# Turned features of tiles 8 to 15 moved inside SBUF in sixteen transfers on two queues, not through DRAM

## The chip, the cores and the metric

The kernel runs on one core of a Trainium2 chip. The metric is the time of one execution in microseconds (us) of device time; a time "of the kernel" is the median of several runs. Beside the timed runs there is one profiled execution, and all durations of single instructions come from it. The engines are called TensorE (PE; PEld is its weight load), VectorE (DVE), ScalarE (ACT), GpSimd (POOL) and SyncE (SP). SyncE and GpSimd each issue DMA transfers from a queue of their own, in order: a transfer at the head of a queue that has to wait holds up all that stand behind it.

## The reference

```python
xn = layernorm(x)                                   # x: 2048 x 512
out = x + A(xn) + B(xn)

def A(x):                                           # linear attention, 32 heads of 16
    q, k, v = heads(x @ wqkv)
    phi_q = cat(softmax(q @ w_phi), softmax(-(q @ w_phi)))    # 32 features a head
    phi_k = cat(softmax(k @ w_phi), softmax(-(k @ w_phi)))
    kv, z = phi_k.T @ v, phi_k.sum(over s)
    o = (phi_q @ kv) / (phi_q @ z + 1e-6)
    return o @ wo

def B(x):                                           # gated MLP, width 688 after the split
    z = gelu(x @ w_in)
    z1, z2 = z[:, :688], layernorm(z[:, 688:])
    return (z1 * (w_sp @ z2 + b_sp[:, None])) @ w_out
```

All is float32. The change concerns `phi_q`, divided by its denominator, on its way to the product with `kv`.

## The kernel before, in words

The 2048 rows are sixteen tiles of 128 rows (NT = 16), and a tile's query features are 128 rows by 1024 features (NF = 1024). Most products are made from three matmuls on split operands (`mm3`, lines 54 to 58: high by high, high by low, low by high), and TensorE works through four stages.

1. Projections of x to v, and to the exponentials of the key and query features. The queries' exponentials and the reciprocals of their sums are stored in DRAM as `e_d` (line 338). The gate inputs z1 are stored too.
2. The second half of the gate input, its layer norm, and its split into operands `B`.
3. The product with `w_sp` in seven partial products (`products`, line 771, tiles named `g`), up to about 489 us. After each of its eight row blocks, `gate` (line 797) makes the gated features u, turns them, and stores them in DRAM as `u_d` and `ur_d` (lines 818 and 820). In this stage the query features of tiles 0 and 1 are turned as well and stored in `q_d` (lines 886 to 891).
4. The projection stage, from about 489 us on: the loop of line 1064 over pairs of tiles, i = 0, 2, ... 14. For each pair TensorE runs `project_u(i)` (u of the first tile by `w_out`, into `pout`), then `attend` (32 small matmuls of line 997, from `kvT` and the turned features `f`, into `po`), then `project_u(i + 1)`, then `project_o` for both tiles (`oT` by `wo`, into the same `pout`). ScalarE copies `pout` to `xr`, of which there are three buffers, and GpSimd adds `xr` to the output in DRAM (line 1030). In between, ScalarE and VectorE split the next u (`uh`, `ul`) and the outcome of `attend` (`oT`, lines 1001 and 1002).

The matmuls of `attend` contract over features, so the features have to stand on partitions: each tile's 128 x 1024 block must be turned. Tiles 2 to 7 are turned on TensorE (lines 974 to 985). Tiles 0, 1 and 8 to 15 are turned on VectorE: one transpose instruction (line 561) turns all 32 x 32 blocks in place, and a DMA then has to carry the blocks to their partitions. For tiles 8 to 15 that is the branch `s >= TQ` of `features` (lines 935 to 940):

- `q_fin` (line 541) divides by the denominator, in seven VectorE instructions with `tmp` as scratch;
- `turn_q` (line 559) transposes `e` into `tmp` (tile name `qtmp`), and four DMAs on GpSimd's queue, one for each block b of 32 partitions, store it in `q_d[s]`, 128 KB each;
- one DMA on SyncE's queue loads `q_d[s]` into the half of the pair's operand tile `f`, 512 KB. It waits for the four stores.

The operand tiles `f` come from `er_pair`, which has three buffers of a pair each. `tmp` and the tile `et`, into which `e_d` is loaded, come from the rotating slots of `xz`.

The order of the work: `ahead(i)` (line 1054) asks, after the `project_o` of tile i, for the load of `et` of tile i + 5, of u of tile i + 4, and for `features(i + 3)`. In line 1087 the last `gate` is put behind pair 6; it stores the u of tiles 14 and 15. `tc.issue_after` puts instructions behind a given one on the same engine. What this does not fix is laid out by a planner, which runs through the program with simulated times (`schedule_with_timeline_sim=True`, line 1121) and from them writes the order of each engine and each queue; on the chip each engine then follows its order strictly, and waits by semaphores.

Of the kernel before, what the change touches and what calls it, by code (L numbers as in the profile page):

```python
# [10 lines left out]
F32 = mybir.dt.float32  # L11
# [7 lines left out]
P = 128  # L19
S, D, H, DH, FH = 2048, 512, 32, 16, 688  # L20
NT = S // P
# [3 lines left out]
NF = 2 * D  # L25
# [3 lines left out]
BL = 32  # L29
# [11 lines left out]
def mixer(ctx: ExitStack, tc: tile.TileContext, x, x_t, wv, wqkT, phi_bd, wo, w_in, wst, b_r, w_out, out):  # L41
    nc = tc.nc
    pe, act, dve, pool, sp = nc.tensor, nc.scalar, nc.vector, nc.gpsimd, nc.sync


    def round_h(eng, h, src):
        if eng is act:
            return act.activation(h, src, AF.Copy).ins  # L48
        return eng.tensor_copy(h, src).ins

    def rest_l(l, src, h, eng=None):
        return (eng or dve).tensor_tensor(l, src, h.bitcast(F32), op=ALU.subtract).ins  # L52
# [18 lines left out]
    def xz_tile(n, dt, name):  # L71
        return xz.tile([P, SL], dt, tag="xz", name=name)[:, :n]

    mid = ctx.enter_context(ExitStack())
    dram = ctx.enter_context(tc.tile_pool(name="dram", bufs=1, space=DRAM))
# [3 lines left out]
    ur_d = dram.tile([NT, 2 * REM, P], F32, name="ur_d")  # L79
    kvT_d = dram.tile([P, D], F32, name="kvT_d")  # L80
    zb_d = dram.tile([P, NF], F32, name="zb_d")
    q_d = dram.tile([NT, P, NF], F32, name="q_d")
    nm_d = dram.tile([NT, ND, P], F32, name="nm_d")

    ident = cst.tile([P, P], F32, name="ident")
# [91 lines left out]
    with ExitStack() as p0:  # L177
# [236 lines left out]
        t = xz_tile(2 * D, F32R, "xT").rearrange("p (a b) -> p a b", a=2)  # L414
        xT.append(t)
        x0, pts = xt.pop(0), []
        for k in range(2):
            pts.append(ps.tile([P, 2, P], F32, tag="mm", name="pt"))
            for c in range(2):
                i = pe.transpose(pts[k][:, c], x0[:, (2 * k + c) * P:(2 * k + c + 1) * P], ident).ins  # L420
            keep(pe=i)
        warm_up(2)
        for cs, pt in zip(halves, pts):
            src = pt.rearrange("p a b -> p (a b)")
            i = round_h(act, t[:, 0, cs], src)
# [7 lines left out]
        p = ps.tile([P, D], F32, tag="mm", name="proj")  # L433
# [7 lines left out]
        p = ps.tile([P, D], F32, tag="mm", name="proj")  # L441
# [18 lines left out]
        p = ps.tile([P, D], F32, tag="mm", name="proj")  # L460
# [80 lines left out]
    def q_fin(et, tmp, zb):  # L541

        e, r, t, w = et[:, :NF], *(et[:, NF + k * 2 * H:NF + (k + 1) * 2 * H] for k in range(3))
        den = et[:, NF + 6 * H:QW]
        dve.tensor_tensor(tmp, e, zb, op=ALU.mult)
        dve.tensor_reduce(t, heads(tmp), axis=AX.X, op=ALU.add)
        dve.tensor_tensor(t, t, r, op=ALU.mult)
        dve.scalar_tensor_tensor(den, pairs(t, 0), EPS_DEN, pairs(t, 1), op0=ALU.add, op1=ALU.add)
        dve.reciprocal(den, den)
        dve.tensor_tensor(w.rearrange("p (h a) -> p h a", a=2), r.rearrange("p (h a) -> p h a", a=2),  # L550
                          den.unsqueeze(2).to_broadcast([P, H, 2]), op=ALU.mult)
        return e, dve.tensor_tensor(heads(e), heads(e), bc(w, 2 * H), op=ALU.mult).ins
# [3 lines left out]
    NB = NF // P  # L556
    QB = NB * BL

    def turn_q(s, dst, e, eng):

        dve.transpose(dst.rearrange("p (m c t) -> p m c t", c=NB, t=BL), e.rearrange("p (c m j) -> p m c j", c=NB, j=BL))
        for b in range(P // BL):
            eng.dma_start(q_d[s, :, b * QB:(b + 1) * QB].rearrange("(m j) w -> j m w", j=BL),
                          dst[b * BL:(b + 1) * BL].rearrange("p (m w) -> p m w", w=QB))

    QC = 4
    NQ = NT // QC
# [45 lines left out]
    with ExitStack() as p1:  # L613
# [44 lines left out]
        for s in range(NE):  # L658
            et = load_q(s, tb.tile([P, QW], F32, name="et") if s else tmp1.tile([P, 4, D], F32, tag="zhl", name="et").rearrange("p a b -> p (a b)")[:, :QW])
            tmp = zw.tile([P, 4, FC], F32, tag="z2", bufs=2, name="qtmp").rearrange("p a b -> p (a b)")[:, :NF]  # L660
            e, _ = q_fin(et, tmp, zb)
# [57 lines left out]
    for s in range(NT):  # L719
        p = zproj((kv_ps_p, zc, zbp, za)[s % 4], s, w2, (0, 1) if s % 2 == 0 else (1, 0))  # L720
# [6 lines left out]
        z = z2[n][:, 2 * (s % 2):2 * (s % 2) + 2]  # L727
# [37 lines left out]
    def load_z1(i):  # L765
        t = gt.tile([P, 2, FH + REM], F32, tag="z1", name="z1t")
        for k in range(2):
            pool.dma_start(t[:, k, :FH], z1_d[2 * i + k])  # L768
        return t
# [27 lines left out]
    def gate(i, cb, z, u, ut, after=None):  # L797
        cb, first, _ = cb
        with tc.issue_after(after or first):
            act.activation(z[:, :, :FH], z[:, :, :FH], AF.Gelu_apprx_tanh)  # L800
        zs = z[:, :, :FH].rearrange("p k (j f) -> p k j f", j=2)
        us = u[:, :, :FH].rearrange("p k (j f) -> p k j f", j=2)
        dve.tensor_tensor(us, zs, cb, op=ALU.mult)
        lo, hi = u[:, :, KF * P:FH], u[:, :, FH:FU].bitcast(F32R)
        dve.tensor_copy(hi, lo)
        rest_l(lo, lo, hi)

        def turn():
            src = ut.rearrange("p k f -> p (k f)")
            m, r = src[:, :2 * KF * P], src[:, 2 * KF * P:]  # L810
            for k in range(2):
                dve.transpose(m[:, k * KF * P:(k + 1) * KF * P].rearrange("p (m c t) -> p m c t", c=KF, t=BL),
                              u[:, k, :KF * P].rearrange("p (c m j) -> p m c j", c=KF, j=BL))
            dve.transpose(r.rearrange("p (k f) -> p k f", k=2), u[:, :, KF * P:])
            eng = pool if i == NP - 2 else sp
            for b in range(0, P, BL):
                w = b // BL * KF * BL
                eng.dma_start(u_d[2 * i:2 * i + 2, :, w:w + KF * BL].rearrange("k (m j) w -> j (k m) w", j=BL),
                              m[b:b + BL].rearrange("p (m w) -> p m w", w=KF * BL))
                eng.dma_start(ur_d[2 * i:2 * i + 2, :, b:b + BL].rearrange("k (a j) t -> j (k a) t", j=BL),  # L820
                              r[b:b + BL].rearrange("p (a t) -> p a t", t=BL))

        return turn

    def slot(name, dt=F32):
        return xz_tile(2 * FH, dt, name)
# [40 lines left out]
    g, es, ets, ft, ep = {}, {}, {}, {}, {}  # L867
    for n in range(NC):
        i = SEQ[n][0]
        if n % NQ == 1 and i < NP - 1:  # L870
            z = load_z1(i)
        products(n, g)
        if n % NQ == NQ - 1 and i < NP - 1:
            c = gt.tile([P, 2, FU], F32, tag="c", name="c")
            cq = c[:, :, :FH].rearrange("p k (j f) -> p k j f", j=2)
            cb = drain(i, g, cq)
            g = {}
        if n + 3 < NC:
            raw[n + 3] = load_a(n + 3)
        if n + 2 < NC:  # L880
            A[n + 2] = prep_a(n + 2, raw.pop(n + 2))
        if n % NQ == NQ - 1 and i < NP - 1:
            turn = gate(i, cb, z, c, z, prep_a.last)
            if i < NP - 2:
                turn()
            if i in (2, 4):
                s = i // 2 - 1
                e, t = (gt.tile([P, 2, FU], F32, tag=tag, name=name).rearrange("p k f -> p (k f)")[:, :NF]
                        for tag, name in (("c", "c"), ("z1", "z1t")))
                pool.dma_start(e, e_d[s, :, :NF])  # L890
                turn_q(s, t, e, pool)
        if n == NC - 4:
            stage_w()
        if n == NC - 3:
            zs = slot("zb", F32R)
            zb, ident_r = zs[:, :NF].bitcast(F32), zs[:, NF:NF + P]
            round_h(act, ident_r, ident)
            sp.dma_start(zb, zb_d)
            uT = [first_gate(0)]
            ets[2] = load_q(2, slot("et"))  # L900
            es[2], last = q_fin(ets.pop(2), slot("qtmp")[:, :NF], zb)
        if n == NC - 2:
            fq = [slot("f")[:, :NF].rearrange("p (k b c t) -> p k b c t", k=2, c=NB // 2, t=BL) for h in range(2)]
            for k in range(2):
                for h in range(2):
                    sp.dma_start(fq[h][:, k], q_d[k].rearrange("p (b h w) -> h p b w", h=2, w=QB // 2)[h])
            t = xz_tile((KF + 1) * P, F32R, "u1")
            us = {1: load_u(1, t[:, :KF * P].bitcast(F32), t[:2 * REM, KF * P:(KF + 1) * P])}
    cb = drain(NP - 1, g, slot("c").rearrange("p (k j f) -> p k j f", k=2, j=2))
    with tc.issue_after(cb[2]):  # L910
        turn()
    mid.close()


# [13 lines left out]
    def features(s):  # L928
        with tc.issue_after(fin[-1]):
            tmp = slot("qtmp")[:, :NF]  # L930
            es[s], ins = q_fin(ets.pop(s), tmp, zb)
        fin.append(ins)
        if s == 3:
            return
        if s >= TQ:
            if s % 2 == 0:
                ft[s] = er_pair("f").bitcast(F32)
            turn_q(s, tmp, es.pop(s), pool)
            sp.dma_start(ft[s - s % 2][:, s % 2], q_d[s])
            return  # L940
        e = es[s]
        if s % 2 == 0:
            ep[s] = er_pair("er")
        es[s] = ep[s - s % 2][:, s % 2]
        lasts[6] = pool.dma_start(es[s].bitcast(F32), e).ins
# [117 lines left out]
    p, nxt = {}, dict(enumerate(uT))  # L1063
    for i in range(0, NT, 2):
# [17 lines left out]
        if i == 2:  # L1082
            with tc.issue_after(lasts[6]):
                z = load_z1(NP - 1)
# [40 lines left out]
```

## Time and profile before

| | before |
|---|---|
| timed runs | 619.74, 620.32, 622.54 us; median 620.32 |
| profiled execution | 618.58 us |
| its span, first to last instruction | 616.8 us |
| mean granted TensorE clock | 0.998 |
| bytes moved by DMA | 109.95 MB |
| SyncE's queue (q1, with hardware descriptors) | 43400 packets, 64.96 MB |
| GpSimd's queue (q0, with software descriptors) | 12656 packets, 38.64 MB |

How to read the views: the page's first part gives the busy time of each engine. The windows view gives it by stretches. A timeline row has the start, the duration, the engine, the line, the operation, and what it writes and reads; several equal instructions in a row are merged ("x4"), and then the duration reaches from the start of the first to the end of the last. "SPq" is SyncE's queue: the duration is that of the issue, not of the transfer. What follows in brackets is how long the engine sat idle before and what ended that. "Landing" is the time from a DMA's issue to its arrival. The chain of waits follows the work that ended last back to its start; "issue" is time in which the engine waited for nothing that the profile can name.

### The profile page before, as it was taken

Reading aid. Unit: us, or ns where it says so; the run is one execution under the profiler, and the core shown is the slowest. Engines: PE = TensorE matmul, PEld = TensorE weight load, DVE = VectorE, ACT = ScalarE, POOL = GpSimd, SP = SyncE. Lnnn points to the kernel's source line nnn. Section 1 sums busy time; section 2 is a strip of 40 time slices with the busy share of each in tenths; the row PEclk is TensorE's granted clock in tenths of the full one; section 3 lists DMA queues with packets and bytes.
Section 4 is the critical chain, followed back from the end, with each engine's and each line's share of the span. In section 5 each row is a group of like instructions: output and inputs, shape, how many; then the busy total and the mean of one; then the engine's idle time right before and its main releaser. Section 6 shows DMA issues by size and latency. Waiting matters only on the chain.

```text
span 616.8 us, 11392 instructions
## 1 busy us (share of the span) xinstructions
PE 607.8 (99%) x4286; PEld 554.4 (90%) x4286; DVE 519.0 (84%) x929; ACT 261.5 (42%) x416; POOL 134.2 (22%) x236
## 2 busy tenths in 40 slices
PE   8999999999999999999999999999999999999996
PEld 7888888888889999999999999999999987777775
DVE  5999999999978398989889896877879999999821
ACT  5653334323523467876434443342435343332221
POOL 4122232232110015442000002000100032344420
PEclk9999999999999999999999999999999999999999
DMA  8557876666446768001463745555566799999772
GB/s 315 192 136 165 227 178 170 159 163 169 125 143 162 255 224 289 2 1 35 149 142 124 191 96 177 135 157 145 165 182 215 214 345 306 322 272 264 188 172 58
DMA packets 58415, 109.95 MB, mean 178 GB/s; under 512 B 12457, under 2 KB 24617, under 8 KB 58121
## 3 DMA queue, kind: packets, MB, share of 16 engines
q1 hardware_dynamic: 43400, 64.96, 34.4%
q0 software_dynamic: 12656, 38.64, 25.1%
q10 hardware_dynamic: 2304, 5.64, 2.3%
q8 instruction: 33, 0.54, 0.3%
q14 instruction: 22, 0.17, 0.1%
HBM read 66.85 MB, written 35.80 MB: 166 GB/s over the span
## 4 chain that ended last, share of the span: by engine, by line
PE 95%; DMA 2%; issue 0%; DVE 0%; ACT 0%; SPq 0%; POOL 0%; DVEq 0%; ACTq 0%; POOLq 0%
PE g L58 11%; PE g L57 11%; PE g L56 11%; PE proj L57 7%; PE proj L56 7%; PE proj L58 7%; PE zps L56 6%; PE zps L57 6%; PE zps L58 6%; PE pout L56 6%; PE pout L58 5%; PE pout L57 5%; PE po L997 1%; DMA wst__2228<-in_w_in 1%; PE kvps L355 1%; PE pout L1011 1%
## 5 line engine op out<-in xcount | busy, mean ns | idle before, releaser
L57 PE MATMUL g<-B,A 128*128 128x344 f32 x448 | 143.3, 320 | 0.0
L56 PE MATMUL g<-B,A 128*128 128x344 f32 x448 | 142.9, 320 | 0.0
L58 PE MATMUL g<-B,A 128*128 128x344 f32 x448 | 140.4, 321 | 0.1
L56 PEld LDWEIGHTS g<-B,A 128*128 128x128 f32 x448 | 84.3, 188 | 0.1
L57 PEld LDWEIGHTS g<-B,A 128*128 128x128 f32 x448 | 84.2, 188 | 0.0
L58 PEld LDWEIGHTS g<-B,A 128*128 128x128 f32 x448 | 83.6, 188 | 0.4 <-DVE A L52 0.4
L48 ACT ACTIVATE A<-S 128x512 fp32r<-128x512 f32 x64 | 39.5, 630 | 78.7 <-DVE S L603 53.7
L56 PE MATMUL proj<-wqk_h,xT 128*128 128x512 f32 x128 | 50.1, 391 | 0.0
L58 PE MATMUL proj<-wqk_h,xT 128*128 128x512 f32 x128 | 49.8, 389 | 0.0
L57 PE MATMUL proj<-wqk_l,xT 128*128 128x512 f32 x128 | 49.8, 389 | 0.0
L123 ACT ACTIVATE e<-e,r_x 128x1024 f32<-128x1024 f32 x26 | 29.8, 1148 | 42.3 <-DVE e L122 41.2
L52 DVE TENSOR_TENSOR A<-S,A 128x512 fp32r<-128x512 f32 x64 | 43.0, 684 | 3.1 <-ACT A L48 2.8
L48 ACT ACTIVATE A<-wf 128x512 fp32r<-128x512 f32 (+1 forms) x64 | 32.9, 516 | 24.9 <-DMA wf<-in_wst 19.0
L56 PE MATMUL zps<-w_0h,xT 128*128 128x344 f32 x128 | 40.9, 320 | 0.1
L57 PE MATMUL zps<-w_1l,xT 128*128 128x344 f32 x128 | 40.8, 319 | 0.0
L57 PE MATMUL zps<-w_0l,xT 128*128 128x344 f32 x128 | 40.8, 319 | 0.0
L58 PE MATMUL zps<-w_0h,xT 128*128 128x344 f32 x128 | 40.8, 318 | 0.0
L56 PE MATMUL zps<-w_1h,xT 128*128 128x344 f32 x128 | 40.7, 318 | 0.0
L58 PE MATMUL zps<-w_1h,xT 128*128 128x344 f32 x128 | 40.6, 319 | 0.0
L52 DVE TENSOR_TENSOR A<-wf,A 128x512 fp32r<-128x512 f32 (+1 forms) x64 | 35.1, 551 | 3.7 <-ACT A L48 3.7
L126 DVE TENSOR_REDUCE sm<-e 128x64 f32<-128x1024 f32 x26 | 31.1, 1199 | 2.5 <-ACT e L123 2.5
L768 POOL DMA_DIRECT2D z1t<-z_d x16 | 8.7, 552 | 108.8 <-DMA wf<-in_wst 71.8
(224 smaller groups left out, 1435.4 us busy)
## 6 DMA issues: line engine op xcount, KB each, us to landing
wf<-in_wst SPq DMA_DIRECT2D x64, 256.0 KB, 3.2
e_d<-e POOLq DMA_DIRECT2D x16, 544.0 KB, 4.8
et<-e_d SPq DMA_DIRECT2D x16, 544.0 KB, 7.2
z_d<-z1f ACTq DMA_DIRECT2D x16, 344.0 KB, 3.1
z1t<-z_d POOLq DMA_DIRECT2D x16, 344.0 KB, 4.3
zacc<-e POOLq DMA_DIRECT2D x10, 512.0 KB, 4.9
u<-u_d SPq DMA_DIRECT2D x15, 320.0 KB, 4.9
xt<-in_x SPq DMA_DIRECT2D x16, 256.0 KB, 4.3
```

Of the source, the lines that this page charges most:

```text
L48: return act.activation(h, src, AF.Copy).ins
L52: return (eng or dve).tensor_tensor(l, src, h.bitcast(F32), op=ALU.subtract).ins
L56: pe.matmul(dst, ah, bh, start=start, stop=False)
L57: pe.matmul(dst, ah, bl, start=False, stop=False)
L58: return pe.matmul(dst, al, bh, start=False, stop=stop).ins
L123: softmax_pair.last = less, act.activation(e, e, AF.Exp, scale=scale).ins
L126: dve.tensor_reduce(sm, heads(e), axis=AX.X, op=ALU.add)
L355: i = pe.matmul(kv_acc[k:k + QP, m // 4], vs[:, m * QP:(m + 1) * QP], e[:, m * HP:(m + 1) * HP], start=first and m < 4 and len(ready) == n ...
L768: pool.dma_start(t[:, k, :FH], z1_d[2 * i + k])
L997: lasts[3] = pe.matmul(po[r][c * QP:(c + 1) * QP, k], kvT[rows, m // 2, cols], fs[m // 4][rows, m // 2 % 2], start=True, stop=True).ins
L1011: lasts[2] = pe.matmul(p, rt, w, start=False, stop=i == NT - 1 and k == 1).ins
```

## The change

For tiles 8 to 15 the four stores to `q_d` and the load from it go. In their place `move_q` copies straight from `tmp` to the operand tile: for each block b of 32 source partitions and each block m of 32 target partitions one DMA of 32 partitions by 256 elements (1 KB each, 32 KB in all). Those with b = 0 and 2 are issued on SyncE's queue, those with b = 1 and 3 on GpSimd's, so a tile has eight on each. Tiles 0 and 1 still go through `q_d`, which shrinks to two tiles. `turn_q` is divided into `turn` and `store_q`, and the function that `gate` returns is now held as `turn_u`.

```diff
-    q_d = dram.tile([NT, P, NF], F32, name="q_d")
+    q_d = dram.tile([2, P, NF], F32, name="q_d")
...
-    def turn_q(s, dst, e, eng):
-
+    def turn(dst, e):
         dve.transpose(dst.rearrange("p (m c t) -> p m c t", c=NB, t=BL), e.rearrange("p (c m j) -> p m c j", c=NB, j=BL))
+
+    def store_q(s, t):
         for b in range(P // BL):
-            eng.dma_start(q_d[s, :, b * QB:(b + 1) * QB].rearrange("(m j) w -> j m w", j=BL),
-                          dst[b * BL:(b + 1) * BL].rearrange("p (m w) -> p m w", w=QB))
+            pool.dma_start(q_d[s, :, b * QB:(b + 1) * QB].rearrange("(m j) w -> j m w", j=BL),
+                           t[b * BL:(b + 1) * BL].rearrange("p (m w) -> p m w", w=QB))
+
+    def move_q(f, t):
+        for b in range(P // BL):
+            for m in range(P // BL):
+                move_q.last = (sp if b % 2 == 0 else pool).dma_start(f[m * BL:(m + 1) * BL, b * QB:(b + 1) * QB],
+                                                      t[b * BL:(b + 1) * BL, m * QB:(m + 1) * QB]).ins
...
                 pool.dma_start(e, e_d[s, :, :NF])
-                turn_q(s, t, e, pool)
+                turn(t, e)
+                store_q(s, t)
...
         if s >= TQ:
             if s % 2 == 0:
                 ft[s] = er_pair("f").bitcast(F32)
-            turn_q(s, tmp, es.pop(s), pool)
-            sp.dma_start(ft[s - s % 2][:, s % 2], q_d[s])
+            turn(tmp, es.pop(s))
+            move_q(ft[s - s % 2][:, s % 2], tmp)
             return
```

More of the change, by code (lines that the diff above doesn't have):

```diff
@@ L882, in mixer @@
         if n % NQ == NQ - 1 and i < NP - 1:
-            turn = gate(i, cb, z, c, z, prep_a.last)
+            turn_u = gate(i, cb, z, c, z, prep_a.last)
             if i < NP - 2:
-                turn()
+                turn_u()
             if i in (2, 4):
@@ L910, in mixer @@
     with tc.issue_after(cb[2]):
-        turn()
+        turn_u()
     mid.close()
```

## The prediction, made before the result was known

> **What bounds the kernel now.** I read the page first: span, busy shares and the chain of waits.
>
> ```profile
> span 616.8 us, 11392 instructions
> ...
> PE 607.8 (99%) x4286; PEld 554.4 (90%) x4286; DVE 519.0 (84%) x929; ACT 261.5 (42%) x416; POOL 134.2 (22%) x236
> ...
> PE 95%; DMA 2%; issue 0%; DVE 0%; ACT 0%; SPq 0%; POOL 0%; DVEq 0%; ACTq 0%; POOLq 0%
> ```
>
> TensorE is busy 99% of the span and is 95% of the chain that ended last. A change that takes no matmul away can win only what TensorE idles: 616.8 - 607.8 = 9.0 us in all, start and end included. The change touches the projection stage (from 489 us on), and there only tiles 8 to 15. So next came the windows, cut from one `po` (line 997) to the next; columns are busy us and count of PE, PEld, DVE, ACT, POOL, then clock, DMA share, GB/s.
>
> ```profile
> 525.48:541.39 15.91, 15.91 (x114) 12.66 (x120) 15.47 (x22) 5.72 (x11) 5.39 (x9) 1.00 0.99 307
> 541.39:555.87 14.48, 14.48 (x99) 11.31 (x105) 14.22 (x24) 5.02 (x8) 5.25 (x9) 1.00 0.98 282
> 555.87:571.92 16.05, 14.47 (x91) 11.26 (x91) 15.78 (x23) 3.84 (x7) 6.61 (x11) 1.00 0.98 273
> 571.92:586.47 14.55, 14.55 (x98) 11.44 (x105) 12.28 (x19) 3.68 (x6) 6.12 (x10) 1.00 0.70 174
> 586.47:600.94 14.47, 14.47 (x98) 11.30 (x105) 2.98 (x5) 3.10 (x6) 4.00 (x6) 1.00 0.76 169
> ```
>
> One window has a hole: the third takes 16.05 us for 14.47 of matmuls. The others are full. The chain, in order of time, names the place:
>
> ```profile
> 569.87 0.47 PE pout L1011 x2
> 570.34 1.58 issue
> 571.92 1.10 PE po L997 x32
> ```
>
> TensorE is ready for the `po` of pair 10 (tiles 10 and 11) at 570.34 and starts at 571.92. No engine is named; the `po` reads `f`, which comes by DMA. The timelines of VectorE (the transposes, line 561), GpSimd and SyncE's queue show how late `f` is:
>
> ```profile
> 538.88 1.24 DVE L561 STREAM_TRANSPOSE qtmp<-et 128x1024 f32<-128x1024 f32 x1
> ...
> 556.93 1.24 DVE L561 STREAM_TRANSPOSE qtmp<-et 128x1024 f32<-128x1024 f32 x1
> ...
> 570.16 1.24 DVE L561 STREAM_TRANSPOSE qtmp<-et 128x1024 f32<-128x1024 f32 x1
> ...
> 585.27 1.25 DVE L561 STREAM_TRANSPOSE qtmp<-et 128x1024 f32<-128x1024 f32 x1
> ```
>
> ```profile
> 558.47 2.25 POOL L563 DMA_DIRECT2D q_d<-qtmp  x4 [4.61 <-DVE qtmp L561]
> ```
>
> ```profile
> 554.72 0.32 SPq L939 DMA_DIRECT2D f<-q_d  x1
> ...
> 558.95 0.48 SPq L820 DMA_DIRECT2D ur_d<-zt  x1
> 560.84 0.34 SPq L538 DMA_DIRECT2D et<-e_d  x1
> 563.60 0.34 SPq L836 DMA_DIRECT2D u<-u_d  x1
> 564.10 0.80 SPq L837 DMA_DIRECT2D rt<-ur_d  x2
> 564.94 0.43 SPq L836 DMA_DIRECT2D u<-u_d  x1
> 565.53 29.80 SPq L939 DMA_DIRECT2D f<-q_d  x5
> ```
>
> The four transposes are those of tiles 9, 11, 13 and 15, the second of each pair; they end at 540.12, 558.17, 571.40 and 586.52. Tile 11's stores are issued from 558.47 to 560.72, its load (the first of the x5) only at 565.53, and `po` starts 6.4 us later. So the way from transpose to operand takes 571.92 - 558.17 = 13.75 us for tile 11. Call it M. What TensorE allows before it stalls is, by pair: 8, 555.87 - 540.12 = 15.75; 10, 570.34 - 558.17 = 12.17; 12, 586.47 - 1.58 - 571.40 = 13.49; 14, 600.94 - 1.58 - 586.52 = 12.84 (the last two with the stall taken out of TensorE's clock). Pair 10 is the tightest, and 13.75 - 12.17 = 1.58 is the hole. If M were the same for every tile, the end would move by max(0, M - 12.17) - 1.58.
>
> **The change, part by part.** Removed, for eight tiles: four stores on GpSimd and one load on SyncE, and SyncE's wait between them. Added: sixteen moves of 32 partitions by 1 KB, eight on each queue, which wait for the transpose itself. The matmuls, and all up to tile 8, stay. The rows for the price come from SyncE's waits, its timeline, the answer for line 831, the answer for `q_d`, the page's DMA issues, and the answer for `er` from 500 us on:
>
> ```profile
> SPq L939 <- DMA q_d<-qtmp: 36.5, 9, 9.4
> ```
>
> ```profile
> 482.88 8.61 SPq L831 DMA_DIRECT2D wof<-in_wo  x16
> ```
>
> ```profile
> DMA to landing us min/median/max: 1.9/3.3/5.2
> ```
>
> ```profile
> L563 POOL DMA_DIRECT2D q_d<-qtmp x32: 550/572/937, 534.6 to 588.5; - x32
> ```
>
> ```profile
> u_d<-zt SPq DMA_DIRECT2D x4, 160.0 KB, 5.1
> ```
>
> ```profile
> DMA to landing us min/median/max: 5.6/7.7/9.6
> ```
>
> The waits of SyncE for `q_d` (36.5 us) go, and nothing that TensorE needs hangs on them but `f`. For the new M: issue on SyncE, 16 small loads in 8.61 us (second), 0.54 each, so 8 x 0.54 = 4.3 us; on GpSimd at the present store's 0.572, 8 x 0.572 = 4.6. Landing: the trace has no 32 KB move inside SBUF. From below, the 64 KB `wof` loads land in 1.9 at the least (third). From above, the 512 KB copy `er<-et`, the one SBUF to SBUF transfer there is, takes up to 9.6 (last). I take 5.1, of the `u_d<-zt` stores: also many small transfers by 32 partitions, in the same crowded stretch, with DMA at 0.98. SyncE stands behind those stores until 558.95 + 0.48 = 559.43, 1.3 after tile 11's transpose. M = 1.3 + 4.6 + 5.1 = 11.0, against 12.17 allowed: the hole closes, by 1.2 us of margin. The ends are 4.3 + 1.9 = 6.2 (hole gone just as well) and 1.3 + 8 x 0.937 + 9.6 = 18.4. For pairs 8, 12 and 14 the same 11.0 is under 15.75, 13.49 and 12.84, so pair 14 is late next. Gain: 1.58.
>
> One row says the queue can choke:
>
> ```profile
> SPq L538 <- DMA f<-q_d: 1.4, 1, 1.4
> ```
>
> The `et` load at 560.84 neither reads nor writes `f`, yet waited 1.4 us for an `f` load: the one at 554.72, exactly eight issues before it. I read this as at most eight transfers in flight on a queue. Tile 11's eight moves then each wait for one of the eight `u_d` and `ur_d` stores. With 5.1 us of landing these are free from 553 + 5.1 on, so this lies within the 1.3 already counted; under slower landings it does not.
>
> On GpSimd the change adds 32 issues net, 32 x 0.572 = 18 us, 4.6 per pair; it is busy 6.61 of 16.05 us in the fullest window. Queued behind its moves are the `out` accumulations, which free the three `xr` buffers:
>
> ```profile
> 551.35 0.92 POOL L1030 DMA_DIRECT2D out<-xr  x1 [0.91 <-ACT xr L1029]
> ```
>
> ```profile
> 566.56 0.60 ACT L1029 ACTIVATE xr<-pout 128x512 f32<-128x512 f32 x1 [1.04 <-PE pout L58]
> ```
>
> ```profile
> out<-xr POOLq DMA_DIRECT2D x15, 256.0 KB, 6.2
> ```
>
> The buffer written at 566.56 is that of the issue at 551.35, which lands at 557.6: 9.0 us of cover, against one tile's moves ahead of it at 4.6. Cost nothing; without cover, up to 4.6 a pair. Behind SyncE's moves stand the loads of `et`, `u` and `rt`; they lose the blocking by `q_d` and gain 4.3 us of issues a tile, so I count nothing.
>
> More transfers mean more waits to pass for who reads `f` or reuses `qtmp`:
>
> ```profile
> L997 PEldq EVENT_SEMAPHORE  x7: 51/51/5757, 489.0 to 598.7; - x7
> ```
>
> ```profile
> L545 DVEq EVENT_SEMAPHORE  x7: 21/50/50, 536.6 to 568.0; - x7
> ```
>
> ```profile
> 546.13 0.69 DVE L52 TENSOR_TENSOR oT<-po,oT 128x512 fp32r<-128x512 f32 x1
> ```
>
> ```profile
> 547.28 0.39 PE L58 MATMUL pout<-woh,oT 128*128 128x512 f32 x1
> ```
>
> At 51 ns each, sixteen waits ahead of a `po` are 0.8 us, passed ahead of the matmuls: the last such wait stands at 598.7, 2.2 us before its `po`. That hides them. On VectorE, sixteen at 50 ns are 0.8 us a tile. It is full until 572 (15.78 of 16.05), and its `oT` ends at 546.82, 0.46 before a matmul reads it; at worst 0.34 is lost there. I take 0 for both: today seven such waits stand at the twelve instructions of line 545 from 500 us on, and no stall comes of them.
>
> Sum: the profiled execution took 618.58 us (1.8 more than its span). 618.58 - 1.58 = 617.0. The three timed runs have a median of 620.32, 1.74 above it; carried along, the forecast is 618.7 us, 0.25% faster. About 0.5%, or 3.1 us, is what a measurement can tell from no change, so the limits are 617.2 and 623.4.
>
> **A rule against the change.** The row `wof` x16 shows transfers that overlap: one after another at 3.3 us they would need 53 us, not 8.61 plus a landing. The Trainium skill, "DMA: Bandwidth & Descriptors", section "Rules for kernel authors", says to put many small transfers together into a large one, since under 64 KB one pays mostly overhead. The Trainium skill, same page, section "Anatomy of one DMA", fits about 2.0 us plus bytes over 436 GB/s for each; by that a 32 KB move is an estimated 2.1 us, and sixteen in a row 33 us. The sum above would be ruined by it only if the fixed part were paid in series, and by `wof` it is not.
>
> **The rivals.**
>
> *The queue's order eats the gain.* The order of SyncE's queue is made by the planner from simulated times. If it puts tile 11's moves where the `f` load of line 939 stands now, behind the `u` and `rt` loads that must wait for the `u_d` round trip, they start at 564.94 + 0.43 = 565.4 instead of 559.4. With eight issues of 4.3 and a landing between 1.9 and 5.1, M is 13.4 to 16.6, at `wof`'s median 14.8: a time of 620.0 to 623.2, most likely 621.4, hardly other than before. For it: the present order. Against: the moves are ready at 558.17, 7 us before that load was issued.
>
> *Slower: the landings choke.* Sixteen small moves go out where the DMA share is 0.98, eight in flight per queue, each held by the one eight before it. Place: the `po` of pair 10. It loses from M = 13.75 on, a landing of 13.75 - 1.3 - 4.6 = 7.85, 1 us for 1 us, up to 18.4 - 13.75 = 4.65: 620.3 to 625.0, and it passes 623.4 at M = 16.85. For it: the landing of 9.6. Against: a tile now moves 512 KB once instead of storing and loading it, and only `wof`'s and `u_d`'s landings are of small transfers.
>
> *Moves that do not overlap at all.* At 3.3 us each, eight on a queue are 26 us a tile and eight tiles 211 us from 534 on, over 140 us late. The `wof` row speaks against it.
>
> *Faster than the hole.* If the timed runs are above the profiled one (619.74 to 622.54) because `f` came still later in them, a shorter route takes that away too, and the time is that of the sum, 617.0. For it: `f` of tile 15 is close as well,
>
> ```profile
> 588.35 6.99 SPq L939 DMA_DIRECT2D f<-q_d  x2
> ```
>
> ```profile
> DMA to landing us min/median/max: 4.8/5.3/5.8
> ```
>
> its load ends its issue at 588.35 + 6.99 = 595.34, 5.6 before its `po` at 600.94, when landings of `f` from `q_d` range over 4.8 to 5.8. Against: nothing shows what those runs did.
>
> **How the numbers follow.** Forecast 0.52; the order eats the gain 0.16; slower 0.13, of it 0.08 over 623.4; no overlap 0.02; faster than the hole 0.17. Faster by over 0.5%: 0.17. Slower: 0.08 + 0.02 = 0.10. Same: 0.73. The range runs from 616.6, a little under 617.0 for scatter, to 622.4, which is M = 15.85: it leaves out about 0.09 of the slower case, 0.03 of the order's, 0.02 without overlap, and 0.04 below.
>
> **What would show it.** Right: no `issue` piece before any `po` from 541 on; windows of 14.5 us for pairs 8 to 14; eight moves of a tile issued in 4 to 5 us on each queue right behind its transpose; the end of the stage 1.6 us earlier, the first 525 us unchanged. The time per move is wrong if landings are over 6.3 us, where the margin of 1.2 is gone. The prediction is wrong if a `po` still waits, if matmuls wait for `oT` or `uh` where they did not before, or if the planner has changed the order of TensorE or VectorE ahead of 534.

## The result, and the profile after

| | before | after |
|---|---|---|
| median of 19 runs each, us | 620.32 (618.21 to 624.37) | 625.63 (622.65 to 631.26) |
| ratio, 95% interval | | 1.0086 [1.0059, 1.0114] |
| profiled execution, us | 618.58 | 627.27 |
| its span, us | 616.8 | 625.5 |
| mean granted TensorE clock | 0.998 | 0.992 |

The changed kernel is slower by 0.9%, where 0.25% faster was forecast. It lies outside the range (616.6 to 622.4) and on the side that had a chance of 0.10. The profiles differ by 8.7 us of span, more than the medians (5.3 us); the table of terms below says why.

The page of the changed kernel: its span, the engines' busy time, and the chain by engine.

```profile
span 625.5 us, 11533 instructions
...
PE 614.3 (98%) x4286; PEld 557.6 (89%) x4286; DVE 519.7 (83%) x929; ACT 262.6 (42%) x416; POOL 147.7 (24%) x268
...
PE 92%; DMA 4%; DVE 2%; issue 1%; ACT 0%; POOL 0%; SPq 0%; POOLq 0%; DVEq 0%; ACTq 0%
```

TensorE has the same 4286 matmuls and is busy 6.5 us longer (614.3 against 607.8), and idles 11.2 us instead of 9.0. So three quarters of the loss is hidden inside "busy". GpSimd has gained 32 instructions, as counted, and its share of the chain is 0%.

The windows of the changed kernel, cut from one `po` to the next and at the end, with the prediction's columns:

```profile
526.69:542.61 15.92, 15.92 (x114) 12.66 (x122) 14.93 (x21) 5.72 (x11) 7.20 (x13) 1.00 0.78 212
542.61:557.08 14.47, 14.47 (x94) 11.30 (x98) 14.22 (x24) 5.00 (x8) 8.10 (x16) 1.00 0.77 205
557.08:573.30 16.22, 14.91 (x93) 11.56 (x94) 15.24 (x22) 3.84 (x7) 8.61 (x17) 1.00 0.96 222
573.30:592.71 19.41, 18.70 (x94) 13.22 (x98) 13.06 (x20) 3.78 (x6) 11.65 (x22) 0.82 0.53 109
592.71:609.15 16.44, 15.72 (x95) 11.56 (x98) 3.04 (x4) 3.21 (x6) 5.34 (x10) 1.00 0.45 81
609.15:625.50 16.35, 11.19 (x85) 9.08 (x85) 2.83 (x5) 1.69 (x3) 0.86 (x1) 0.91 0.25 55
```

The first two windows are those of before (15.91, 14.48). From the third on each is longer: 16.22 for 16.05, 19.41 for 14.55, 16.44 for 14.47, 16.35 for 15.86. These four make 0.17 + 4.86 + 1.97 + 0.49 = 7.49 us. The other 1.21 lie ahead of 526.69, in a wait of 1.27 us of a transpose on TensorE for `er<-et` at 521. No instruction of the change stands there. That wait is missing in the profiles of e1, e3, e6 and e7 (below), and in e7's a wait of 1.43 stands at another place nearby, so it counts as scatter between executions.

What happens at pair 10 stands in the timeline of TensorE of the changed kernel:

```profile
573.28 1.07 PE L1005 MATMUL po<-f,kvT 64*32 64x256 f32 x16 [1.31 <-DMA f<-qtmp]
575.06 0.80 PE L56 MATMUL pout<-woh,oT 128*128 128x512 f32 x1 [0.71 <-ACT oT L48]
...
576.21 1.93 PE L1005 MATMUL po<-f,kvT 64*32 64x256 f32 x16
578.66 0.63 PE L57 MATMUL pout<-wu,uh 128*128 128x512 f32 x1
```

Four things are to be seen. The hole is still there, 1.31 us. The 32 matmuls of `po`, one row before ("x32"), have become two groups of sixteen. Between the groups stand two matmuls of `project_o`, which need `oT` of the first half and wait 0.71 us for ScalarE to make it. And behind the second group matmuls start 0.43 apart (578.66 to 579.09, the next row) where they started 0.23 apart before the hole. In pair 12 the same groups stand at 592.64 and 595.09, with a wait of 0.72; in pairs 8 and 14 there is no gap, but `po` takes longer:

```profile
609.08 1.52 PE L1005 MATMUL po<-f,kvT 64*32 64x256 f32 x32
```

That is 1.52 for the 1.09 to 1.10 of before. TensorE's order in the program is unchanged up to pair 8. From there the planner has sorted the sixteen matmuls that read the first two of the four partition blocks of `f` ahead of the sixteen that read the last two, where the code, and the kernel before, alternate between them. The moves have made `f` arrive in sixteen pieces; a likely reason is that in the planner's times the last blocks land later.

How late the moves are is to be seen in the timelines of VectorE, SyncE's queue and GpSimd of the changed kernel, for tile 11:

```profile
558.14 1.24 DVE L560 STREAM_TRANSPOSE qtmp<-et 128x1024 f32<-128x1024 f32 x1
```

```profile
562.51 0.72 SPq L843 DMA_DIRECT2D u<-u_d  x1
563.28 0.96 SPq L538 DMA_DIRECT2D et<-e_d  x1
565.07 0.32 SPq L843 DMA_DIRECT2D u<-u_d  x1
565.49 5.17 SPq L570 DMA_DIRECT2D f<-qtmp  x8
```

```profile
559.67 4.05 POOL L570 DMA_DIRECT2D f<-qtmp  x8 [2.37 <-DVE qtmp L560]
```

GpSimd sends its eight 0.3 us after the transpose has ended (559.38). SyncE sends its eight only from 565.49: behind the `u_d` stores, as foreseen, and behind two loads of u and one of `et`, as the rival of the queue's order had it. M is 573.28 - 559.38 = 13.90 us, as much as the 13.75 of before.

The answer for the tile `f` of the changed kernel has what one move costs:

```profile
L570 SPq DMA_DIRECT2D f<-qtmp x64: 507/589/1919, 535.1 to 595.8; - x64
L570 POOL DMA_DIRECT2D f<-qtmp x64: 496/506/930, 535.4 to 597.3; - x64
...
DMA to landing us min/median/max: 1.7/3.9/7.2
```

### The profile page after: what moved, and what is told of

The parts are those of the page before. It is cut to its first block, busy times and chain, and to the rows that moved or that the text cites. A ratio compares the mean times of both kernels' runs of the same rounds, so it can differ in the third digit from the quotient of the medians.

```text
span 625.5 us, 11533 instructions
## 1 busy us (share of the span) xinstructions
PE 614.3 (98%) x4286; PEld 557.6 (89%) x4286; DVE 519.7 (83%) x929; ACT 262.6 (42%) x416; POOL 147.7 (24%) x268
## 4 chain that ended last, share of the span: by engine, by line
PE 92%; DMA 4%; DVE 2%; issue 1%; ACT 0%; POOL 0%; SPq 0%; POOLq 0%; DVEq 0%; ACTq 0%
PE g L58 11%; PE g L57 11%; PE g L56 11%; PE proj L56 7%; PE proj L57 7%; PE proj L58 7%; PE zps L56 6%; PE zps L57 6%; PE zps L58 6%; PE pout L56 4%; PE pout L57 4%; PE pout L58 4%; PE po L1005 2%; PE kvps L355 1%; DMA u<-u_d 1%
## 5 line engine op out<-in xcount | busy, mean ns | idle before, releaser
L570 POOL DMA_DIRECT2D f<-qtmp x64 | 33.0, 611 | 27.1 <-DVE qtmp L560 20.0
```

The source lines that it names most:

```text
L570: move_q.last = (sp if b % 2 == 0 else pool).dma_start(f[m * BL:(m + 1) * BL, b * QB:(b + 1) * QB], t[b * BL:(b + 1) * BL, m * QB:(m + 1) ...
```

## The experiments

Theory: the loss comes from TensorE's new order, that is from the halves, the two matmuls between them and the waits in the middle; the moves themselves are harmless, and the hole is a matter of what stands ahead on SyncE's queue. Rivals: the landings of 128 small moves choke the DMA engines; or the sixteen waits per `po` cost by their number, in any order. All ratios are to the kernel before, run on the same chip, whose median was 620.83 (29 runs) beside e1, e6, e3 and e5, and 620.39 (35 runs) beside the others. They stand as measured, with a 95% interval, and are not quite the quotients of the medians.

### e1: the moves stay, TensorE's order is put back

```diff
+            with tc.issue_after(lasts[3]) if m else ExitStack():
                 lasts[3] = pe.matmul(po[r][...], kvT[...], fs[m // 4][...], start=True, stop=True).ins
...
+            with tc.issue_after(lasts[2]):
                 project_o(i + k, oT, p.pop(i + k))
```

> The changed kernel, with TensorE's order put back by hand: the po matmuls of a pair follow each other as written (row halves alternating), and project_o stands behind project_u of the second tile. Queues and moves stay as changed. Theory O (the loss is TensorE's order: po sorted by row halves, 0.43 us a pair in four pairs, and two project_o matmuls put between the halves of pairs 10 and 12, 0.7 us each): every po takes 1.0 us again, no wait for oT between the halves, clock 0.997 or more, and the time is that of the kernel before, ratio 0.998 to 1.002; the wait for f before pair 10 stays at about 1.3 us, because SyncE's queue is as it was. Theory L (the loss is the late moves, which stand behind the u loads on SyncE): only the 3 us of order go, ratio 1.004 to 1.008, with a wait of over 2 us before pair 10.

Measured: 620.49 us, ratio 0.9986 [0.9958, 1.0014]; profiled 618.74. The loss is gone with all 128 moves in place, so these are not what costs. The hole stays, in TensorE's timeline of e1:

```profile
571.53 1.56 PE L1006 MATMUL po<-f,kvT 64*32 64x256 f32 x32 [1.18 <-DMA f<-qtmp]
```

The `po` of pairs 8, 12 and 14, which have no hole ahead, are back at 1.09. And the number of waits is not what makes them long: the answers for the `po` line give, for the changed kernel and for e1,

```profile
L1005 PEldq EVENT_SEMAPHORE  x44: 51/51/51, 488.7 to 609.4; - x44
```

```profile
L1006 PEldq EVENT_SEMAPHORE  x45: 51/51/51, 488.5 to 597.9; - x45
```

about the same number (7 before). What differs is the place. In the trace of the changed kernel four of these wait instructions stand in the middle of each `po`, ahead of the second half: for pair 14, whose `po` starts at 609.08, at 609.10, 609.21, 609.31 and 609.42. They take 51 ns but start 0.11 us apart. In the trace of e1 the eleven waits of pair 8 run from 551.64 to 552.73, and its `po` starts at 555.81: the long matmuls of the product before are still running then and cover them.

### e6: the other way round, only SyncE's queue is set right

```diff
-                move_q.last = (sp if b % 2 == 0 else pool).dma_start(...).ins
+                ins = (sp if b % 2 == 0 else pool).dma_start(...).ins
+                if b % 2 == 0:
+                    move_q.last = ins
...
+            with tc.issue_after(move_q.last) if i + 4 >= NT - 3 else ExitStack():
                 us[i + 4] = fetch_u(i + 4)
```

The loads of u for tiles 13 to 15 go behind the SyncE moves asked for before them.

> The changed kernel, with one thing altered: on SyncE the loads of u of tiles 13 to 15 are put behind the moves that were asked for before them, so tile 11's moves go out after the u_d stores and one et load and not after two u loads. TensorE's order stays split. Theory O: the wait for f before pair 10 falls below 0.5 us, but po stays at 1.45 us in four pairs and the 0.7 us waits for oT stay, so the time stays over the kernel before: ratio 1.001 to 1.006. Theory L: most of the loss goes, ratio 0.997 to 1.001.

Measured: 623.75, ratio 1.0036 [1.0012, 1.0061]; profiled 621.82. TensorE's timeline of e6:

```profile
570.61 1.07 PE L1007 MATMUL po<-f,kvT 64*32 64x256 f32 x16
572.40 0.50 PE L56 MATMUL pout<-woh,oT 128*128 128x512 f32 x1 [0.72 <-DMA f<-qtmp]
...
573.06 1.07 PE L1007 MATMUL po<-f,kvT 64*32 64x256 f32 x16
574.06 0.50 PE L56 MATMUL pout<-wu,uh 128*128 128x512 f32 x1
```

The hole is gone, the split is not. (The row names a move of `f` as what ended the 0.72; the matmul reads `oT`, and in pair 12 of e6 the same 0.72 is put down to ScalarE's `oT`.) This is the split's price without the hole: 574.06 - 570.61 = 3.45 us from the first `po` to the next product of u, for 572.95 - 571.92 = 1.03 before; 0.46 of it are the two matmuls that only changed place, so 1.96 are lost. The windows of e6 say the same, and that the clock stayed at 1.00:

```profile
570.61:587.05 16.44, 15.72 (x92) 11.56 (x91) 14.37 (x21) 3.88 (x7) 11.09 (x22) 1.00 0.81 172
587.05:603.53 16.48, 15.76 (x92) 11.58 (x91) 3.03 (x4) 3.28 (x6) 5.89 (x11) 1.00 0.49 88
```

They replace 14.55 and 14.47 of before. In the changed kernel the first of them took 19.41 at a clock of 0.82: 19.41 - 16.44 = 2.97 us more, with the same instructions of TensorE in it.

### e3: both, the order and the queue

The edits of e1 and e6 together.

> Both at once: the changed kernel with TensorE's order put back and SyncE's u loads behind the moves. Theory O with the queue as second cause: no wait for f, no wait for oT, windows of 14.5 us for pairs 8 to 14, so the forecast's 1.6 us are won: ratio 0.995 to 0.999, profiled time 616.5 to 617.5. Theory L: the same as without TensorE's order put back, within 0.2%.

Measured: 618.07, ratio 0.9951 [0.9928, 0.9974]; profiled 618.56, where 616.5 to 617.5 was expected. SyncE's queue in e3, where tile 11's moves now go before u (its transpose ended at 558.56):

```profile
562.28 1.31 SPq L538 DMA_DIRECT2D et<-e_d  x1
563.70 4.97 SPq L570 DMA_DIRECT2D f<-qtmp  x8
568.76 0.53 SPq L845 DMA_DIRECT2D u<-u_d  x1
```

A good part of the hole is left, in TensorE's timeline of e3:

```profile
570.77 0.59 PE L1008 MATMUL po<-f,kvT 64*32 64x256 f32 x2
571.74 1.09 PE L1008 MATMUL po<-f,kvT 64*32 64x256 f32 x30 [0.37 <-DMA f<-qtmp]
```

TensorE counts as idle for only 0.37 us, but the first two matmuls of the `po` start 0.97 us ahead of the other thirty, and the window of pair 10 takes 15.45 and not the 14.5 that was expected. M is 571.74 - 558.56 = 13.18 us in this profile, still over the 12.17 allowed: the moves start 5.14 us after the transpose, behind the `u_d` stores, which end at 561.92, and one load of `et`. So the ratio came out as expected, but this profile does not show the whole hole closed. The win needs two orders that the change itself does not set.

### e10: the halves stay, only the two matmuls between them are put back

```diff
+            with tc.issue_after(lasts[2]):
                 project_o(i + k, oT, p.pop(i + k))
```

> The changed kernel, with project_o put behind project_u of the second tile, so that nothing of it stands between the halves of po; po itself stays sorted by row halves, with the four wait instructions in its middle, and SyncE's queue stays as changed. If the two inserted project_o matmuls and the fall of TensorE's clock that goes with them are the larger part: po still takes 1.45 us in four pairs (+1.7 us), the wait for f before pair 10 stays at 1 to 2 us, clock falls no oftener than in the kernel before: ratio 1.001 to 1.004. If the waits in the middle of po are the larger part, and the inserted matmuls are harmless: ratio 1.006 to 1.009.

Measured: 621.2, ratio 1.0013 [0.9985, 1.0041]; profiled 621.10. TensorE's timeline of e10, pair 12:

```profile
587.97 1.52 PE L1005 MATMUL po<-f,kvT 64*32 64x256 f32 x32
```

All four `po` take 1.52 to 1.74 and nothing waits for `oT`. So the waits in the middle of `po` cost 1.52 - 1.09 = 0.43 where no other matmul stands between the halves, and putting the two matmuls back saves the other 1.5 of the split's 1.96 us. That does not make 0.43 a part of the 1.96: e5, next, has the split without these waits and loses as much. The ratios of e10 and e1 differ by 0.0027, or 1.7 us, which is 4 x 0.43; their intervals overlap, so this rests on the rows.

### e5: the kernel before, with the changed kernel's order of TensorE

The route through DRAM stays. `attend` runs the sixteen matmuls of one half, settles its `oT`, then runs the other sixteen in pairs 8 to 14; in 10 and 12 the two matmuls of `project_o` stand between.

```diff
+        for n, m in enumerate([*range(0, H // 2, 2), *range(1, H // 2, 2)] if halves else range(H // 2)):
+            if halves and n == H // 4:
+                settle(0)
+                between(oT)
```

> The kernel before, way through DRAM and all, with only TensorE's order of the changed kernel written in by hand: po by row halves in pairs 8 to 14, two project_o matmuls between the halves in pairs 10 and 12. Theory O: po takes 1.45 us in four pairs (+1.7 us) and TensorE waits 0.7 us for oT twice (+1.4 us): about 3 us slower, ratio 1.004 to 1.006, and up to 1.010 in runs in which the hole of 1.6 us and the 0.7 us next to it bring TensorE's clock down. Theory L: nothing is late that was not late before, ratio 0.999 to 1.002.

Measured: 629.14, ratio 1.0117 [1.0083, 1.0151]; profiled 629.11. So the order makes the loss without any move. TensorE's timeline of e5:

```profile
556.10 1.12 PE L1006 MATMUL po<-f,kvT 64*32 64x256 f32 x32
...
574.98 1.93 PE L1006 MATMUL po<-f,kvT 64*32 64x256 f32 x16 [4.31 <-issue]
...
595.35 1.07 PE L1006 MATMUL po<-f,kvT 64*32 64x256 f32 x16
597.13 0.50 PE L1027 MATMUL pout<-woh,oT 128*128 128x512 f32 x1 [0.71 <-ACT oT L48]
...
597.80 1.07 PE L1006 MATMUL po<-f,kvT 64*32 64x256 f32 x16
598.80 0.51 PE L56 MATMUL pout<-wu,uh 128*128 128x512 f32 x1
```

The first row separates order and waits: halves one after the other cost 1.12 - 1.09 = 0.03 where no waits stand between them. The last four rows are pair 12, at a clock of 1.00 and with no wait instruction inside the `po`: 598.80 - 595.35 = 3.45 us from the first `po` to the next product of u, the same as in e6. So the two matmuls between the halves make the whole 1.96 by themselves, and the four waits add nothing where TensorE waits for `oT` anyway. The loss in all is over what was expected, though (ratio up to 1.010): the hole before pair 10 has grown to 4.31, where the `f` load is issued at 566.68 and `po` starts 8.3 us later, and the clock falls behind it. Why the load landed so late in this version was not found out. So e5 shows the price of the split, but its median is not that price.

### e7: the kernel before, with only SyncE's queue set right

```diff
-            sp.dma_start(ft[s - s % 2][:, s % 2], q_d[s])
+            features.last = sp.dma_start(ft[s - s % 2][:, s % 2], q_d[s]).ins
...
+            with tc.issue_after(features.last) if i + 4 >= NT - 3 else ExitStack():
                 us[i + 4] = fetch_u(i + 4)
```

> The kernel before, with the way through DRAM, and only SyncE's u loads of tiles 13 to 15 put behind the f loads that were asked for before them. If it is the queue's order that makes the hole before pair 10: the f load of tile 11 goes out at about 565 us or earlier, the hole falls to 0.5 us or less, the clock stays at 0.997 or more, and the ratio is 0.995 to 0.998, about that of the version with moves, the new queue order and TensorE's old order. If the two trips through DRAM are what makes f late: the hole stays over 1 us, ratio 0.999 to 1.001, and only the direct moves win.

Measured: 617.33, ratio 0.9953 [0.9927, 0.9979]; profiled 618.35. No move is made inside SBUF, and the gain is that of e3. The order of the work on TensorE, VectorE, ScalarE and GpSimd is the same in the traces of e7 and of before, so nothing but SyncE's order is left to explain it. SyncE's queue and TensorE's timeline of e7:

```profile
561.13 0.34 SPq L538 DMA_DIRECT2D et<-e_d  x1
566.56 0.34 SPq L939 DMA_DIRECT2D f<-q_d  x1
567.00 0.38 SPq L836 DMA_DIRECT2D u<-u_d  x1
```

```profile
571.41 1.09 PE L997 MATMUL po<-f,kvT 64*32 64x256 f32 x32
```

The hole is gone (from pair 8 on the windows take 14.47, 14.47 and 14.48), but not in the way that was expected, for the load of `f` is not issued earlier: 566.56 is 7.25 us after this profile's transpose (559.31), 565.53 was 7.36 after it before, and e7's row waits 5.0 us for the stores to `q_d`. But it lands within 571.41 - 566.56 = 4.85 us, where before `po` started 6.39 after the issue. What has changed are its neighbours: before, two loads of u and two of `rt` were issued in the 2 us ahead of it and were on their way together with it. So, as far as these two profiles go, the hole of the route through DRAM is made by the traffic that the queue puts ahead of `f`, more than by the waiting in the queue. In e5, with the queue of before, the landing was later still, so these neighbours are not all that sets it.

### e9 and e8: the last gate later, without and with the moves

The `u_d` stores that stand ahead of tile 11's moves come from the last `gate`. Both kernels put it one pair later; e8 has the edits of e1 as well.

```diff
-    GATE_LAST = 6
+    GATE_LAST = 8
```

> The kernel before, with the way through DRAM, and only the last gate one pair later. If the place of the gate is what makes tile 11 late, and not the way through DRAM: no hole before pair 10, clock 0.997 or more, ratio 0.993 to 0.998, as with the moves. If the way through DRAM is too long even so: a hole of 0.5 us or more before one of the pairs 10 to 14, ratio 0.998 to 1.000.

Measured (before, with the late gate): 623.36, ratio 1.0033 [1.0, 1.0067], above both ranges; profiled 624.61. TensorE's timeline of e9:

```profile
590.88 1.74 PE L997 MATMUL po<-f,kvT 64*32 64x256 f32 x28 [4.49 <-issue]
```

The hole has gone from pair 10 to pair 12 and is three times as long: SyncE's queue in e9 shows what the load of `f` stands behind there:

```profile
575.40 1.45 SPq L820 DMA_DIRECT2D ur_d<-zt  x1
580.98 0.34 SPq L836 DMA_DIRECT2D u<-u_d  x1
...
583.23 8.14 SPq L939 DMA_DIRECT2D f<-q_d  x2
```

The queue issues nothing from 576.85 to 580.98, when u may be loaded back; `f` follows at 583.23 and `po` 7.65 us later. In the trace the last store of `f`'s data into `q_d` has landed at 580.66, so the queue's order makes up to 583.23 - 580.66 = 2.57 us of the delay, and the slow landing the rest.

> The changed kernel with TensorE's order put back, and the last gate (gelu, product, transposes and the u_d stores of tiles 14 and 15) one pair later, behind pair 8 and not pair 6, so that tile 11's transpose comes about 4 us earlier and its moves stand ahead of the u_d stores. If the hole is the last thing to be won: no wait for f, clock 0.997 or more, ratio 0.993 to 0.997. If the late gate brings the u of tile 14 late in turn: a wait for uh at about 585 us, ratio over 0.998.

Measured (the moves, TensorE's order put back, the late gate): 618.45, ratio 0.9947 [0.9917, 0.9977]; profiled 619.24. TensorE's timeline of e8 has no hole before pair 10 and this in pair 12, behind the first two matmuls of its `po`:

```profile
586.87 1.09 PE L1006 MATMUL po<-f,kvT 64*32 64x256 f32 x30 [0.31 <-issue]
```

As in e3, those two start early (585.97), and TensorE loses more than the 0.31 it counts as idle: the window of pair 12 takes 15.41 for 14.47, 0.94 more. Here the direct moves do something that the route through DRAM does not: about 1 us lost for 4.49. But no version with them beats e7, which is the smallest edit of all. At about 0.995, e3, e7 and e8 cannot be told apart by their times; in the profiles only e7 has no rest of the hole.

## Why the prediction was wrong

The step that failed is the sentence "The matmuls, and all up to tile 8, stay." They stay in number, not in order. The prediction let the planner choose only SyncE's queue anew. Among its signs of being wrong it named matmuls that wait for `oT`, which is what came, and a new order of TensorE ahead of 534, while the order changed from pair 8 on; it gave this no term, no price and no chance. What the runs showed in its place: the new order costs 1.89 and 1.97 us in pairs 10 and 12 and 0.43 to 0.49 in pairs 8 and 14, and putting it back (e1) takes the loss away. A second step failed beside it: M was 13.90 us and not 11.0, so the hole did not close. Point by point:

- **The sum.** Forecast was -1.58. The profile has these terms, each from the windows and the e-runs named:

| term | us | from |
|---|---|---|
| hole before pair 10: 1.31 for 1.58 | -0.27 | timeline; not closed |
| waits in the middle of `po`, pairs 8 and 14 | +0.92 | 0.43 by e10; 0.49 is the last window's whole excess |
| split of pair 10, without the clock | +1.89 | e6's window: 16.44 - 14.55 |
| split of pair 12 | +1.97 | 16.44 - 14.47; e6 has 16.48 |
| clock at 0.82 in one window | +2.97 | 19.41 against e6's 16.44 |
| wait at 521, scatter | +1.21 | absent in e1, e3, e6, e7 |
| sum | +8.7 | 625.5 - 616.8 = 8.7 |

The sum can be tried on the timed runs. Without scatter and clock it is 8.7 - 1.21 - 2.97 = 4.5 us. Executions with a mean clock of 0.997 or more have medians of 623.84 (changed) and, in the two sets beside the experiments, 619.66 and 619.50 (before): 4.2 to 4.3 us. The rest, up to the medians' 5.3, is the clock (last section).

- **M = 11.0 by SyncE behind the `u_d` stores.** The place was right (TensorE waits for `f` of tile 11, nowhere else), M was 13.90. The argument that the moves are ready 7 us before that load was issued did not hold against the order of the queue. The rival *the queue's order* had this: a start 565.4 - 558.17 = 7.2 us after the transpose (measured 565.49 - 559.38 = 6.1), M from 13.4 to 16.6. It had a chance of 0.16 and, alone, would have left the time where it was. The 1.3 us behind the stores was too small as well: tile 10's own moves now stand ahead of them on the queue, and they end at 562.40, 3.0 us after the transpose (3.4 in e3, whose M is 13.18 without the u loads). And by the prediction's own reading of eight transfers in flight, the last of the eight stores, issued at 558.95, would have held the eighth move until 558.95 + 5.1 = 564.05, which is not within the 1.3.
- **The price of a move.** 0.54 on SyncE (589 ns median, eight in 5.17 us) and 0.572 on GpSimd (506 ns, eight in 4.05), landing 5.1 (3.9 median, 7.2 at the most): near enough, and the landing was even better. *The landings choke*, which needed 7.85, is thus refuted here, by e1 too (6.4 at the most; only e8 has a longer one, 8.8), and *no overlap at all* is as well. SyncE's eight of tile 11 were issued and landed in 573.28 - 565.49 = 7.8 us. The Trainium skill, "DMA: Bandwidth & Descriptors", section "Rules for kernel authors", warns of many transfers under 64 KB as mostly overhead: the runs show the overhead as issue time and waits, and no loss from the transfers.
- **Sixteen waits counted as hidden.** Right for waits ahead of the first matmuls (e1), wrong for those in the middle of a `po`: four instructions of 51 ns made 0.43 us (e10), since they start 0.11 us apart and nothing long runs there to cover them.
- **VectorE and GpSimd at nothing.** Right: VectorE's windows are no fuller (14.93, 14.22, 15.24 for 15.47, 14.22, 15.78), and nothing on TensorE waits for `xr`.
- **The value of closing the hole.** e7 gains 3.06 us (617.33 against 620.39), not 1.58. The rival *faster than the hole* supposed that `f` comes still later in the timed runs; what the runs show is another addition, the clock. Among executions at a clock of 0.997 or more the gain is 619.50 - 617.33 = 2.2 us; the 0.6 above 1.58 that is left there is not explained. Its row of landings (4.8 to 5.8) was misread: it takes in four loads of `f` from stage 3, and tile 11's own load let the `po` start only 6.39 us after its issue.

Left open: why `f` lands so late in e5, why e6 has no rest of the hole where e3 has one, and why the clock falls in one execution of a kernel and not in another. That the planner sorted the halves because it had the last blocks landing later is likely, not shown.

## What to carry to other kernels

Where a planner orders the engines, splitting one transfer into pieces can change the order in which its readers run: look at the reader's order first, and pin it when the pieces arrive, before counting microseconds of transfer. Waits that are free ahead of a group of short matmuls are paid in the middle of it, unless the engine waits there for something else anyway. And when an engine waits for a load, look at what is queued and in flight ahead of it before building another route: here one pinned order on SyncE's queue, with the old route, was worth as much as any version of the new one.

## What the runs showed of the hardware

A hole of a little over a microsecond can cost more than itself. The windows of the changed kernel behind the hole of pair 10:

```profile
571.97:573.28 1.31, 0.01 (x1) 0.03 (x1) 1.31 (x2) 0.09 (x1) 0.00 (x0) 1.00 0.70 130
573.28:576.21 2.93, 2.22 (x18) 0.96 (x19) 2.58 (x4) 0.60 (x1) 2.60 (x6) 0.73 0.76 190
576.21:578.07 1.86, 1.86 (x17) 0.58 (x16) 0.00 (x0) 0.00 (x0) 1.86 (x5) 0.50 0.99 194
...
580.00:582.00 2.00, 2.00 (x7) 1.62 (x6) 1.93 (x4) 0.00 (x0) 0.00 (x0) 0.63 0.21 54
582.00:584.00 2.00, 2.00 (x10) 1.62 (x10) 1.00 (x2) 0.74 (x1) 0.00 (x0) 1.00 0.21 52
```

The column before the last two is the granted clock: 1.00 through the hole, then down to 0.50 (in the trace's record of the clock for 6.83 us, from 574.65 to 581.48), then 1.00. Matmuls that start 0.23 us apart start 0.43 apart in it; that is the busy time which the page hides. Every profile also has such a stretch at its end, behind the last products (0.92 in before's last window, 600.94 to 616.80); it alone leaves the mean clock of an execution at 0.997 or more in the profiles here. In the profile of before the hole of 1.58 was not followed by a fall, so the hole is not enough by itself; but the fall goes with holes. In the profiles of e5 and e9, with holes of 4.31 and 4.49, it comes as well, for 10.24 and 3.41 us in their records of the clock. The mean clock was under 0.997 in 25 of 64 executions of before (hole 1.58 in its profile), 10 of 19 of the changed kernel (1.31), 5 of 12 of e1 (1.18), 5 of 12 of e10 (1.24), 7 of 12 of e9 and 5 of 6 of e5, and in 1 of 48 of e3, e6, e7 and e8, whose profiles have TensorE idle for no more than 0.37 at a time before or in a `po`, the waits of e6 for `oT` aside. Those are 0.72, so they alone do not do it. In before's 64 executions those under 0.997 have medians of 623.95 and 622.98 in the two sets, the others 619.66 and 619.50: 4.3 and 3.5 us dearer. With 25 of 64 at about 4 us, a hole of 1.58 costs an estimated 1.58 + 0.39 x 4 = 3.1 us on the mean, about what e7 gained. That the fall is caused by the hole is thus borne out by counts over ten kernels; no run sets the clock by itself. The Trainium skill, "TensorE: Matmul & The Clock Gate", section "What's actually happening", gives a half-rate state after an idle window of about 3.4 us that runs freely against the program. The factor 0.50 and the chance from execution to execution agree with that, and so do the stretches of 6.83, 10.24 and 3.41 us, which are two, three and one times 3.41; the length of the idling does not, since TensorE idled only 1.31 us and then 0.71 here.
